# A linear/sliding-window attention stack with its backward pass: the dense backward stages rewritten with TensorE transposes, one fused first half and staggered tiles, weights loaded and transposed once

## The chip, the cores and the metric

The kernel runs on one core of one Trainium2 chip. The metric is device time in microseconds (us), as the median of the timed executions; less is better. A core has five engines that run their own instruction streams and wait for each other through semaphores: TensorE (PE, matmuls, with its weight loads shown apart as PEld), VectorE (DVE), ScalarE (ACT), GpSimd (POOL) and SyncE (SP). DMAs are started from the streams of SP, ACT and POOL and carried by 16 shared DMA engines; each stream works strictly in order, so a DMA or an instruction that waits holds up all that stands behind it on its engine. The row "PEclk" of the profile is the TensorE clock that was granted, as a share of full speed.

## The reference

A forward pass of four residual layers A, B, A, B over x of 2048 tokens by 640 features (32 heads of 20), and its gradients. Both kinds normalise, project to q, k, v, mix and project back; A and B have one set of weights each, used twice.

```
def _A_ref(x, wqkv, wo):                      # linear attention
    q, k, v = split_heads(x @ wqkv)
    phi = lambda t: jnp.where(t > 0, t + 1, jnp.exp(t)) + 1e-6
    pq, pk = phi(q), phi(k)
    kv = jnp.einsum("bhsd,bhse->bhde", pk, v)
    z = jnp.einsum("bhsd->bhd", pk)
    o = jnp.einsum("bhqd,bhde->bhqe", pq, kv) / (jnp.einsum("bhqd,bhd->bhq", pq, z)[..., None] + 1e-6)
    return merge_heads(o) @ wo
def _B_ref(x, wqkv, wo):                      # causal softmax attention, window of 256
    ...
x = A_x
x = x + _A_ref(_layernorm(x), A_wqkv, A_wo)
x = x + _B_ref(_layernorm(x), B_wqkv, B_wo)
x = x + _A_ref(_layernorm(x), A_wqkv, A_wo)
x = x + _B_ref(_layernorm(x), B_wqkv, B_wo)
outputs: x, d/dA_x, d/dA_wqkv, d/dA_wo, d/dB_wqkv, d/dB_wo for grad_out
```

## The kernel before, in words

Tokens are worked in 16 tiles of 128 rows (`TT`). All stages run one after the other on the core; the layers are numbered 0 (A), 1 (B), 2 (A), 3 (B). Within a stage the program is written tile by tile, and a scheduler that comes with the language lays each engine's instructions in an order of its own: it may move an instruction ahead of one that is written earlier if their data allow it.

1. Forward: `seg_first` does the first half of layer 0, then `seg_pair` twice does the rest of an A layer and the B layer behind it. Each `seg_pair` loads its weights anew (`load_w` for W and Wo of both kinds). `permute_w` writes a copy Wp of the B weights to DRAM at the very start.
2. `seg_do_first` (L645): for layer 3, dO = grad_out times the transposed Wo, scaled by row sums, and written to DRAM as rows (dO) and transposed (dOT). grad_out comes in transposed by DMA.
3. `seg_attention_bwd` (L666) of layer 3, then of layer 1: 128 units of 4 heads by 128 queries, each with two score products, exp, a mask on POOL, dS on DVE, half of the dS blocks transposed by TensorE and half by DMA, and three groups of products. In layer 1 the stage also carries the weight gradients of layers 3 and 2 (`wgrad`) as filler matmuls, `rate` of them at each of two places in a step; what is left over is drained after it. The results of a head group (16 tiles) are collected in one buffer `dqkv_o` and stored by one DMA; in layer 1 there is one such buffer, in layer 3 two.
4. The dense stages behind each attention. `seg_B_to_A` (L854): per tile, d(hn) = dqkv times the transposed Wqkv of B (`dh`, 30 matmuls of 320 columns), the backward of the normalisation, which updates the running gradient `car` in SBUF, then dO of the A layer below (`load_gT`, `A_do`, 10 matmuls), and every four tiles the products pq^T dN that sum into the gradient of the state (`band_products`, added up in SBUF by DVE). `seg_A_to_B` (L876): `close_A_bwd` masks that sum and transposes it, then per tile dq, dk, dv of the A layer (`A_dqkv`), `dh` with A's weights, and for layer 2 also dO of the B layer below (`B_do`). Every operand that a matmul needs transposed is transposed by DMA from the SP queue (`tr`): dqkv (15 blocks of 128 by 128), the gradient gT (5), dN (6), pk and v (5 each), the dO slab (8), and at the head of each stage the weights (75 blocks for Wqkv, 25 for Wo).
5. At the end the weight gradients of layers 1 and 0, added to those of 3 and 2.

The weights for step 4 are made by these lines, called in each dense stage:

```
elif name == "WT":
    t = pool.tile([P, self.QTT, D], BF, name=f"WT{kind}")
    self.tr(t, self.Wp if kind == 1 else self.Wqkv[kind])
```

## Time and profile before

| | |
|---|---|
| median of 3 executions | 2997.4 us (2982.85 to 3011.03) |
| the profiled execution, its own time | 2989.97 us |
| its span (first to last instruction) | 2988.3 us |
| mean granted TensorE clock | 0.794 |
| busy: PE, DVE, ACT, POOL | 2283.8, 1444.5, 1166.9, 765.0 us |
| DMA: packets, bytes | 1016354, 526.67 MB |

The stages in the profiled execution, by the first and last matmul of each: forward to 870 us, dO of layer 3 to 948 (its loads for the attention last to about 976), attention backward of layer 3 to 1353, its dense stages 1402 to 1804, attention backward of layer 1 from 1825 to 2390, left-over weight gradients to 2433, dense stages to 2768, last weight gradients from 2790 to the end. A window's line in the profile gives, after its length, the busy time of PE, PEld, DVE, ACT and POOL with the number of instructions, the granted clock, the mean busy share of the DMA engines (which may pass 1 where packets queue) and GB/s. In a line of waits stand the total, the number of times and the longest, in us.

### The profile page before, as it was taken

To read this page: it belongs to the slowest core of one execution; us is meant where nothing else is said; L and a number is where in the kernel's file an instruction comes from. 1 tells how busy PE (TensorE), PEld (TensorE's weight loads), DVE (VectorE), ACT (ScalarE), POOL (GpSimd) and SP (SyncE) were. 2 spreads that over 40 slices of the span, in tenths; PEclk is the share of its full clock that TensorE was granted. 3 is DMA by queue.
4 is the path that set the end of the run, shared out by engine and by line. 5 is a ranking of instruction groups with operands and counts; after the bars stand their busy time and mean duration, and the time that the engine had idled before them with its cause. 6 is when DMAs were issued, how large, how long until landed. Compare 5 with 4: busy or idle time off the path is not lost. (4 is left out here: it accounts for less than half of the span.)

```text
span 2988.3 us, 65913 instructions
## 1 busy us (share of the span) xinstructions
PE 2283.8 (76%) x26624; PEld 1393.9 (47%) x26624; DVE 1444.5 (48%) x3114; ACT 1166.9 (39%) x2161; POOL 765.0 (26%) x1282
## 2 busy tenths in 40 slices
PE   4689987499853899992746675996899868467689
PEld 3445654245431566662533342564566535244345
DVE  4455654344315666671754563554455427445212
ACT  3347765168740777770101112554555401011000
POOL 0124443146531333331221111222222212111000
PEclk9889997689956555555977785897899889678899
DMA  8698883799859777758978998678776598789776
GB/s 193 207 178 183 187 178 95 173 181 191 191 160 243 173 121 134 130 97 158 187 165 164 216 212 253 147 167 144 175 149 152 144 202 180 161 163 204 250 249 194
DMA packets 1016354, 526.67 MB, mean 176 GB/s; under 512 B 818928, under 2 KB 989936, under 8 KB 1014000
## 3 DMA queue, kind: packets, MB, share of 16 engines
q1 hardware_dynamic: 783984, 204.94, 42.6%
q10 hardware_dynamic: 221312, 280.80, 30.7%
q0 software_dynamic: 10752, 36.71, 5.2%
q8 instruction: 208, 3.41, 0.5%
q14 instruction: 98, 0.80, 0.1%
HBM read 187.40 MB, written 154.63 MB: 114 GB/s over the span
## 5 line engine op out<-in xcount | busy, mean ns | idle before, releaser
L746 DVE TENSOR_TENSOR ds<-sp,e 128x768 bf16<-128x768 f32 (+2 forms) x512 | 463.8, 906 | 418.1 <-PE sp L712 368.2
L726 ACT ACTIVATE e<-sp 128x768 bf16<-128x768 f32 (+2 forms) x512 | 394.7, 773 | 367.0 <-PE sp L712 258.8
L940 PE MATMUL wg<-wg_r,wg_l 128*128 128x320 bf16 (+1 forms) x2240 | 428.4, 336 | 98.5 <-DMA wg_r<-dqkv 32.6
L349 ACT ACTIVATE e<-s 128x768 bf16<-128x768 f32 (+2 forms) x512 | 372.7, 773 | 99.7 <-PE s L347 74.3
L577 PE MATMUL d<-WT,dqkvT 128*128 128x320 bf16 x1920 | 313.3, 328 | 126.6 <-DMA dqkvT<-dqkv_t 72.9
L730 POOL TENSOR_SCALAR_AFFINE_SELECT e<-e 128x512 bf16<-128x512 bf16 x256 | 162.6, 635 | 703.0 <-issue 538.9
L940 PEld LDWEIGHTS <-wg_l 128*128 128x128 bf16 x2240 | 213.7, 102 | 235.1 <-issue 91.3
L577 PEld LDWEIGHTS <-dqkvT 128*128 128x128 bf16 x1920 | 202.5, 107 | 225.3 <-DMA dqkvT<-dqkv_t 76.0
L352 POOL TENSOR_SCALAR_AFFINE_SELECT e<-e 128x512 bf16<-128x512 bf16 x256 | 162.9, 636 | 361.2 <-ACT e L349 357.6
L712 PE MATMUL sp<-KT,QT 32*128 32x384 bf16 (+2 forms) x1024 | 211.8, 411 | 47.1 <-DVE dO_t L533 15.3
L579 ACT ACTIVATE dh_junk<-d 128x320 bf16<-128x320 f32 x128 | 56.0, 437 | 476.9 <-PE d L577 471.8
L712 PE MATMUL sp<-VT,dOT 32*128 32x384 bf16 (+2 forms) x1024 | 212.2, 408 | 32.7 <-DMA dOT<-dOT 15.4
L522 PE MATMUL d<-WoT,gT 128*128 128x320 bf16 x640 | 121.8, 349 | 141.5 <-DMA gT<-car 109.2
L218 PE MATMUL d<-W,ln_hnT 128*128 128x320 bf16 x960 | 161.2, 323 | 56.6 <-DMA ln_hnT<-ln_hn 51.4
L203 PE MATMUL d<-Wo,oT 128*128 128x320 bf16 x640 | 129.8, 329 | 76.4 <-DMA Wo<-in_A_wo_dram 45.6
L306 PE MATMUL d<-W,ln_hnT 128*128 128x480 bf16 x640 | 178.8, 401 | 2.8 <-DVE o_t L293 2.7
L347 PE MATMUL s<-ring 32*128 32x128 bf16 x2880 | 158.0, 230 | 25.8 <-ACT e L349 25.0
L755 PE MATMUL tp<-ident,ds 128*128 128x128 bf16 x1440 | 168.5, 272 | 0.5
L581 DVE CUSTOM_DVE_ANT_0 dh_junk<-d,hn_ld 128x320 bf16<-128x320 f32 x128 | 62.3, 487 | 193.6 <-ACT dh_junk L579 193.4
L522 PEld LDWEIGHTS <-gT 128*128 128x128 bf16 x640 | 66.7, 110 | 189.6 <-DMA gT<-car 120.1
L767 PEld LDWEIGHTS <-ds 128*128 128x128 bf16 x2880 | 105.9, 101 | 100.5 <-issue 97.4
L355 POOL TENSOR_SCALAR_AFFINE_SELECT e<-e 128x512 bf16<-128x512 bf16 x224 | 144.9, 647 | 0.0
(123 smaller groups left out, 3424.5 us busy)
## 6 DMA issues: line engine op xcount, KB each, us to landing
qkvT<-ring ACTq DMA_DIRECT2D x32, 768.0 KB, 5.8
dqkv<-dqkv_o ACTq DMA_DIRECT2D x16, 960.0 KB, 6.1
dqkv<-dqkv_t ACTq DMA_DIRECT2D x32, 480.0 KB, 5.0
wg_r<-dqkv ACTq DMA_DIRECT2D x12, 1280.0 KB, 9.1
wg_r<-dqkv ACTq DMA_DIRECT2D x8, 1920.0 KB, 10.2
hn<-ln_hn ACTq DMA_DIRECT2D x64, 160.0 KB, 3.0
qk<-qk_flat ACTq DMA_DIRECT2D x64, 160.0 KB, 3.5
wg_l<-hn ACTq DMA_DIRECT2D x4, 2560.0 KB, 10.4
```

Source lines behind the costliest of these rows:

```text
L218: nc.tensor.matmul(ps, lhsT=hnT[:, k, :], rhs=W[:, k, ci * HD:(ci + 1) * HD], start=(k == 0), stop=(k == self.DT - 1))
L306: nc.tensor.matmul(ps, lhsT=hnT[:, k, :], rhs=W[:, k, ci * 480:(ci + 1) * 480], start=(k == 0), stop=(k == self.DT - 1))
L349: nc.scalar.activation(ev[:, 2 * half:2 * half + 2], ps[:, :, 0:nkt * P].rearrange("p h (i q) -> p h i q", q=P), ACT.Exp, scale=self.c_att)
L352: nc.gpsimd.affine_select(out=ev[:, :, nkt - 1, :], in_=ev[:, :, nkt - 1, :], compare_op=ALU.is_ge, fill=0.0, base=0, pattern=[[0, 4], [1, ...
L522: self.nc.tensor.matmul(ps, lhsT=gT[:, k, :], rhs=WoT[:, k, c * self.HD:(c + 1) * self.HD], start=(k == 0), stop=(k == self.DT - 1))
L577: nc.tensor.matmul(ps, lhsT=dT[:, k, :], rhs=WT[:, k, cs], start=(k == 0), stop=(k == self.QTT - 1))
L712: nc.tensor.matmul(ps[:, j, 0:nkt * P], lhsT=slabs[g][ta][r0:r0 + HP, b * P:(b + 1) * P], rhs=slabs[g][tb][r0:r0 + HP, k0 * P:(k0 + nkt) * P],
L726: nc.scalar.activation(ev[:, 2 * half:2 * half + 2], ps[:, :, 0:nkt * P].rearrange("p h (i k) -> p h i k", k=P), ACT.Exp, scale=c_att)
L730: nc.gpsimd.affine_select(out=ev[:, :, nkt - 1, :], in_=ev[:, :, nkt - 1, :], compare_op=ALU.is_ge, fill=0.0, base=0, pattern=[[0, 4], [-1 ...
L746: nc.vector.tensor_tensor(out=dv[:, hs], in0=ps[:, :, 0:nkt * P].rearrange("p h (i k) -> p h i k", k=P), in1=ev[:, hs], op=ALU.mult)
L755: nc.tensor.transpose(tp[:, i * P:(i + 1) * P], ds_of[u][:, (nb + i) * P:(nb + i + 1) * P], self.ident)
L940: nc.tensor.matmul(ps, lhsT=lhs[:, tt, rows], rhs=rhs[:, tt, 0:w], start=(tt == 0), stop=(tt == TT - 1))
```

## The change

- **Weights.** W and Wo of both kinds are loaded once, in `seg_first`, and kept for the forward pass. A new generator `flip_w` transposes the four weights once (10 DMA transposes of 15 blocks, 2 of 25) and writes them to DRAM (WT_d, WoT_d); the dense stages read them back with plain DMAs (`dense_weights`). `flip_w` is written as a side job of layer 3's attention; the weights' read follows it there, and in layer 1's attention it follows the filler.
- **Dense stages.** `seg_B_to_A` and `seg_A_to_B` become one function `seg_dense_bwd` with two loops. The gradient, dN, dq, dk/dv and the dO slab are transposed by TensorE against an identity matrix into PSUM (`flip`) and copied to SBUF, nearly all by ACT. Only dqkv of the B layer, pk and v are still transposed by DMA. dq of the A layer is made in the first loop, next to its dO, and the band sums stay in two PSUM banks over all 16 tiles. Each loop runs a plan of small steps at different tile offsets.
- **Work between engines.** The normalisation's backward (`ln_bwd`) reads PSUM once, by ACT (scaled, with the row sum), and goes on from SBUF; one addition and one multiplication of two tensors per tile go to POOL, which did none before; full-width operations (640) take the place of two halves (320).
- **Attention backward.** The factor c_att moves from the dO slab to the dS operation on DVE (tensor_tensor becomes scalar_tensor_tensor). `dqkv_o` becomes two half-size buffers, stored from the POOL queue. The filler rate in layer 1 goes from 5 to 6.

```
+    def flip_w(self, pool):
+        for kind, w in ((1, self.Wp), (0, self.Wqkv[0])):
+            t = pool.tile([P, self.QTT, D], BF, name="wt")
+            for k in range(DT):
+                self.tr(t[:, :, k * P:(k + 1) * P], w[k * P:(k + 1) * P, :])
+                yield
+            self.dma(self.WT_d[:, kind], t, self.nc.sync)
+            yield
...
+            self.tr(t[:, kind * DT:(kind + 1) * DT, :], self.Wo[kind])
...
+        self.dma(self.WoT_d, t[:, 0:2 * DT, :].rearrange("p (k d) f -> p k d f", k=2), self.nc.sync)
...
+    def flip(self, src, n, dst, pt, eng, first=0):
+        for i0 in range(0, n, 8):
+            k = min(8, n - i0)
+            tp = pt.tile([P, 1024], BF, name="t")
+            for i in range(k):
+                c = (first + i0 + i) * P
+                nc.tensor.transpose(tp[:, i * P:(i + 1) * P], src[:, c:c + P], self.ident)
+            v = tp[:, 0:k * P].rearrange("p (i q) -> p i q", q=P)
+            (eng[(i0 // 8) % len(eng)])(dst[:, i0:i0 + k, :], v)
...
         t = pw.tile([P, D], F32, name="do_o")
-        nc.vector.tensor_mul(t, dst, o)
+        nc.gpsimd.tensor_tensor(out=t, in0=dst, in1=o, op=ALU.mult)
...
+    def ln_bwd(self, l, tt, ps, hn, pw):
...
+        nc.scalar.activation(dhs.rearrange("p (c f) -> p c f", c=2), ps[:, :, 0:HD], ACT.Copy, scale=rs,
+                             accum_out=sm[:, 0:1])
...
+        nc.vector.tensor_tensor_reduce(out=junk, in0=dhs, in1=hn, scale=1.0, scalar=0.0,
+                                       op0=ALU.mult, op1=ALU.add, accum_out=sm[:, 1:2])
...
+        nc.gpsimd.tensor_tensor(out=u, in0=dhs, in1=g, op=ALU.add)
...
+        nc.vector.tensor_scalar_mul(ab, sm, -1.0 / D)
...
+        nc.scalar.activation(t2, hn, ACT.Identity, scale=ab[:, 1:2], bias=ab[:, 0:1])
+        nc.vector.tensor_add(g, u, t2)
...
-                nc.vector.tensor_tensor(out=dv[:, hs], in0=ps[:, :, 0:nkt * P].rearrange("p h (i k) -> p h i k", k=P),
-                                        in1=ev[:, hs], op=ALU.mult)
+                nc.vector.scalar_tensor_tensor(
+                    out=dv[:, hs], in0=ps[:, :, 0:nkt * P].rearrange("p h (i k) -> p h i k", k=P),
+                    scalar=c_att, in1=ev[:, hs], op0=ALU.mult, op1=ALU.mult)
...
-                if kt == TT - 1:
-                    self.dma(self.dqkv_d[l][:, :, g * 12 * DH:(g + 1) * 12 * DH], outs.pop(g))
+                if kt % OH == OH - 1:
+                    self.dma(self.dqkv_d[l][:, kt - OH + 1:kt + 1, g * 12 * DH:(g + 1) * 12 * DH], outs.pop(g),
+                             nc.gpsimd)
...
+    def dense_weights(self, l, pool):
+        w = [self.load_w(pool, 1, "WT"), self.load_w(pool, 0, "WoT"), pool.tile([P, 6, self.D], BF, name="mbdT")]
+        self.dma(w[2], self.sv[l - 1]["mbdT"])
+        return w
...
+                plan = ((fetch, 2), (dh0, 0), (flip_g, -1), (flip_dN, -2), (dh1, 0), (dO, -1), (dq_band, -2), (flip_dq, -3))
+                for s in range(-2, TT + 3):
+                    for f, d in plan:
+                        if 0 <= s + d < TT:
+                            f(s + d)
...
+                dmbd, dmbdT = self.close_A_bwd(bands, pb, pt)
...
+                tail = ((flip_g, -1), (dO, -1), (flip_dO, -2)) if a > 0 else ()
+                plan = ((fetch, 4), (fetch2, 2), (dh0, 0), *tail[:1], (flip_dkv, 1), (dh1, 0), *tail[1:2], (dkdv, 2),
+                        *tail[2:])
...
+                if l == 3:
+                    it = before(self.flip_w(self.pool(s3, "fwt", side="right")))
+                    self.seg_attention_bwd(l, None, 0, 3, side=it)
...
-                    self.seg_attention_bwd(l, it, 5, 2, 1)
-                    self.drain(it)
...
+                    it = before(both())
+                    self.seg_attention_bwd(l, it, 6, 2)
+                self.drain(it)
+                self.seg_dense_bwd(l, w)
```

In the plans, `fetch` starts a tile's loads and transposes, `dh0` and `dh1` are the two halves of `dh` (15 matmuls each), `dO` the 10 matmuls of dO with their DVE and POOL work, `dq_band` dq and the 10 band products, `dkdv` dk and dv, and the `flip` steps the TensorE transposes.

How the scheduler lays this, at two places. First the SP queue between the last forward tiles and the dO stage of layer 3; `oT<-o_b` is the last transposes of the forward pass, `gT` and `WoT` what the first matmul of the dO stage waits for. Before:

```order
L127 DMA_TRANSPOSE oT<-o_b 128x5x128 x4
L127 DMA_TRANSPOSE gT<-in_grad_out_dram 128x5x128 x2
L127 DMA_TRANSPOSE WoT_14160<-in_B_wo_dram 128x5x640
L127 DMA_TRANSPOSE gT<-in_grad_out_dram 128x5x128 x3
L127 DMA_TRANSPOSE dOT_ring_14158<-do_slab_14152 128x8x128
```

And now, where `wt` is the tile of `flip_w`:

```order
L129 DMA_TRANSPOSE wt<-Wp 128x15x128
L129 DMA_TRANSPOSE oT<-o_b 128x5x128
L129 DMA_TRANSPOSE wt<-Wp 128x15x128 x4
L129 DMA_TRANSPOSE WoT_14150<-in_B_wo_dram 128x5x640
L129 DMA_TRANSPOSE gT<-in_grad_out_dram 128x5x128
L123 DMA o_ld<-o_109 128x640
```

The first five transposes of `flip_w` stand ahead of WoT and gT. The other seven and the three stores of the transposed weights are spread over the same stage's gT transposes; behind the first dS transposition of the attention there is none.

Second, one tile on DVE in the first dense loop. Before (`dh` of one tile with `A_do` of the tile before it):

```order
L587 TENSOR_SCALAR dh_ab<-dh_ab,rs_97 128x2
L533 TENSOR_TENSOR dN<-d,rinv_100 128x320
L589 TENSOR_SCALAR dh_t_23602<-hn_ld,dh_ab 128x640
L537 TENSOR_TENSOR do_o<-dN,o_ld 128x640
L590 TENSOR_TENSOR car<-dh_t_23556,dh_t_23602 128x640
L539 TENSOR_REDUCE do_s<-do_o 128x32
L581 ISA dh_junk_23658,dh_sm<-d,hn_ld 128x320
```

And now, the whole step of a tile (`dh_s` is ACT's copy of the product, `dh_u` and `do_o` are made by POOL, `dh_t` by ACT):

```order
L595 ISA dh_junk,dh_sm<-dh_s,hn_ld 128x640
L595 ISA dh_sm 128x1
L558 TENSOR_TENSOR dN<-d,rinv_100 128x640
L600 TENSOR_SCALAR dh_ab<-dh_sm 128x2
L918 TENSOR_TENSOR dq_t<-d,dphi 128x640
L566 TENSOR_REDUCE do_s<-do_o 128x32
L603 TENSOR_TENSOR car<-dh_u,dh_t_23801 128x640
L894 CAST dN<-do_s 128x32
```

The reduction that waits for POOL's do_o now stands ahead of the addition into car, and the cast behind both.

413 lines of the change are left out of this document (224 added, 189 removed).

## The prediction

> **What bounds the kernel now.** I read the page first (PE busy 76% of the span, but its clock swings), then a table of the stages, then the waits inside the dense stages, then the timeline at their seams. The table: window, length, busy PE, PEld, DVE, ACT, POOL, granted clock, DMA share, GB/s.
>
> ```profile
> 870.00:948.00 78.00, 30.41 (x164) 16.99 (x166) 44.53 (x121) 0.00 (x0) 11.45 (x19) 0.74 0.93 232
> 948.00:1353.00 405.00, 370.39 (x6063) 236.49 (x6063) 258.79 (x329) 281.39 (x447) 147.03 (x240) 0.50 0.70 136
> 1353.00:1402.00 49.00, 0.52 (x9) 0.34 (x7) 0.00 (x0) 0.36 (x1) 5.51 (x11) 0.50 1.11 190
> 1402.00:1547.00 145.00, 106.20 (x801) 73.34 (x799) 102.60 (x260) 16.91 (x64) 28.59 (x57) 0.89 0.77 160
> 1547.00:1586.00 39.00, 7.60 (x46) 3.90 (x46) 5.96 (x16) 1.51 (x4) 6.97 (x13) 0.50 1.02 222
> 1586.00:1804.00 218.00, 152.40 (x948) 90.29 (x946) 126.46 (x362) 27.46 (x92) 28.22 (x52) 0.80 0.96 191
> 1825.00:2390.00 565.00, 494.21 (x7213) 305.16 (x7212) 273.58 (x349) 296.54 (x491) 147.17 (x241) 0.87 0.73 164
> 2390.00:2433.00 43.00, 21.10 (x118) 12.71 (x117) 1.48 (x3) 2.13 (x5) 5.31 (x10) 0.81 1.16 246
> 2433.00:2578.00 145.00, 108.81 (x800) 74.62 (x800) 101.86 (x260) 16.91 (x64) 26.52 (x54) 0.88 0.75 158
> 2578.00:2610.00 32.00, 7.77 (x44) 3.72 (x44) 5.85 (x15) 1.51 (x4) 5.32 (x10) 0.50 1.01 208
> 2610.00:2768.00 158.00, 114.31 (x788) 70.36 (x788) 79.45 (x231) 26.78 (x90) 23.96 (x38) 0.82 0.90 178
> ```
>
> The dense stages take 1353 to 1804 (451 us) and 2390 to 2768 (378 us). The seams (49, 39, 43 and 32 us) are nearly empty on every engine while the DMA engines are full. Inside, a tile takes 145/16 = 9.1, 218/16 = 13.6 and 158/16 = 9.9 us. What PE waits for there is transposed operands:
>
> ```profile
> PE d L577 <- DMA dqkvT<-dqkv: 48.5, 1, 48.5
> PE d L522 <- DMA gT<-car: 49.6, 12, 7.7
> PE d L577 <- DMA dqkvT<-dqkv_t: 25.1, 5, 9.1
> ```
>
> So the bound is the DMA transposition, in latency per tile and in weights per seam, and the change takes most of it away.
>
> **Forward.** The first output projection of each pair stands idle for a weight:
>
> ```profile
> 125.27 1.23 SPq L127 DMA_TRANSPOSE oT<-o_t  x1
> 142.62 2.83 PE L203 MATMUL d<-Wo,oT 128*128 128x320 bf16 x10 [23.47 <-DMA Wo<-in_A_wo_dram]
> 559.35 2.82 PE L203 MATMUL d<-Wo,oT 128*128 128x320 bf16 x10 [22.14 <-DMA Wo<-in_A_wo_dram]
> oT<-o_t SPq DMA_TRANSPOSE x32, 4.0
> ```
>
> With Wo there, what is late next is its other operand oT: issued at 125.3, 4.0 to landing, so 129.3 in place of 142.6, 13 us. The second wait is as long, so I take 13 again: **-26** (bounds -15, if the tiles behind it give half back, and -47, both waits whole). The earlier loads (4 MB more) stand behind x on the same queue at the start; I cost them at nothing, because the first matmul waits for W there too, and W now comes sooner.
>
> **dO of layer 3.** Written as a side job of the attention, `flip_w` is laid by the scheduler entirely in front of it: 5 transposes ahead of WoT and gT, 7 between the gT, three stores among them. 10 x 15 + 2 x 25 = 200 blocks; the price of one from
>
> ```profile
> 1541.46 16.74 SPq L127 DMA_TRANSPOSE WT<-in_A_wqkv_dram  x1
> q10 hardware_dynamic: 221312, 280.80, 30.7%
> ```
>
> 75 blocks in 16.74 us are 0.223 each: 45 us. The stores, twice 2.46 and once 1.64 MB, go at what the plain queue q10 shows: 280.8 MB in 30.7% of 2988 us are 306 GB/s: 21 us. Against these 66 us the stage has little room: its DMA share is 0.93, and 1.11 is the fullest that a seam shows, so 0.18 x 78 = 14 us. **+52**. Low: +22, if only half of the transposes' time lands on the path. High: +98, with 10 us of SP standing still behind each of two stores (the next `wt` reuses the tile) and the 3.3 MB of WT and WoT, 11 us, ahead of the attention's own rows on ACT's queue.
>
> **A step of the first dense loop.** Durations per instruction come from
>
> ```profile
> L579 ACT ACTIVATE dh_junk<-d 128x320 bf16<-128x320 f32 x128 | 56.0, 437 | 476.9 <-PE d L577 471.8
> L579 ACT ACTIVATION_READ_ACCUMULATOR dh_junk<-d 128x1 f32 x128 | 24.9, 194 | 0.0
> L761 ACT COPY dsT<-tp 128x768 bf16<-128x768 bf16 (+1 forms) x128 | 98.8, 772 | 31.4 <-PE tp L755 25.5 <-DMA po1w<-wg_o 0.9
> L590 DVE TENSOR_TENSOR car<-dh_t,dh_t 128x640 bf16<-128x640 f32 x64 | 52.2, 816 | 0.1
> L539 DVE TENSOR_REDUCE do_s<-do_o 128x32 f32<-128x640 f32 x64 | 52.0, 812 | 0.5
> L323 DVE COPY qk_flat<-qk_slab 128x640 bf16<-128x640 bf16 x64 | 25.8, 413 | 34.4 <-ACT qk_slab L316 34.0
> L598 DVE CAST dN<-do_s 128x32 bf16<-128x32 f32 x32 | 5.7, 177 | 0.3
> L730 POOL TENSOR_SCALAR_AFFINE_SELECT e<-e 128x512 bf16<-128x512 bf16 x256 | 162.6, 635 | 703.0 <-issue 538.9
> 1448.43 4.24 PE L577 MATMUL d<-WT,dqkvT 128*128 128x320 bf16 x30
> 1444.04 1.65 PE L577 MATMUL d<-WT,dqkvT 128*128 128x320 bf16 x11
> 1445.79 0.44 ACT L579 ACTIVATE dh_junk<-d 128x320 bf16<-128x320 f32 x1 [2.14 <-PE d L577]
> 1733.61 2.85 PE L522 MATMUL d<-WoT,gT 128*128 128x320 bf16 x10 [6.86 <-DMA gT<-car]
> 2380.51 0.51 PE L755 MATMUL tp<-ident,ds 128*128 128x128 bf16 x6
> 2747.03 0.30 PE L623 MATMUL d<-mbdT,dNT 32*128 32x320 bf16 x1
> 2749.25 4.24 PE L577 MATMUL d<-WT,dqkvT 128*128 128x320 bf16 x30
> ```
>
> PE's own work, at full clock: 40 matmuls of 320 columns at 4.24/30 = 0.141 are 5.65; 16 transposes at 0.51/8 = 0.06 (spacing, without the last one's tail) 1.0; dq 1.0 of the 2.2 us that dq, dk and dv take from 2747.03 to 2749.25; 10 band products 0.5, half of the 0.1 that those 22 matmuls average, as most have fewer columns: **8.1 us**.
>
> The step is not PE's, though. dN of tile t-1 must be transposed before `dh1` of the next tile, and DVE makes it behind work that needs `dh1` of this tile. The new wait is DVE's reduction for POOL's do_o; car and the cast are queued behind it, and PE's transposes of both, with `dh1` behind them, wait for these. The loop, from the end of one `dh1` to the end of the next: ACT's copy of 640 (between 437 for 320 and 772 for 768: 0.68) and its accumulator 0.19; DVE's product with hn 0.82; dN 0.82; POOL's do_o; the reduction 0.81; car 0.82; the cast 0.18; 11 transposes 0.65; 15 matmuls 2.12; eight changes of engine at 0.1 (PE's matmuls end at 1445.69, ACT begins at 1445.79). dq, the small ab and ACT's dh_t lie beside POOL's time. No row has a two-tensor operation on POOL. With one input, 635 ns for 512 make 0.79 for 640, and twice that is 1.6; below stands DVE's 0.82, above twice the 1.6, 3.2. I take 1.6, the row's price once per input: **9.5 us**. The page "GPSIMD Engine Reference" of the Trainium skill (section 3.1) gives 4497 ns for a two-tensor addition over 2048 on GpSimd against 2293 on VectorE; scaled to 640 that is an estimate of 1.4 us, by which the step would be 9.3. No run here shows it yet.
>
> **A step of the second loop.** For layer 2 the same chain with the slab's copy (0.41) in place of the cast and 15 transposes (0.9) in place of 11: 9.5 + 0.23 + 0.25 = **10.0**; PE's own 5.65 + 23 x 0.06 + 1.25 = 8.3. For layer 0 there is no dO and no such chain: PE's 30 x 0.141 + 10 x 0.06 + 1.25 = 6.1, plus a tenth for waits: **6.7**.
>
> **Seams.** The weights are in SBUF before the attention ends, so the first matmul waits for 15 blocks: 4.0 for the 5 of oT plus 10 x 0.22, about 7 us. Between the loops the last tile runs through its whole stagger: car (6.3 of the chain), its transposes and copy 1.0, dO 1.5, the dN chain 3.4, transposes, copy, dq and bands 2.6, five masked pieces with ACT copies of 0.77 about 5, dk, dv and their transposes 3.6, hops 1.6: 25 us.
>
> Layer 3's dense part: 7 + 16 x 9.5 + 25 + 16 x 10.0 + 9 for the last tile = 353, against 451: **-98**. Layer 1's: 7 + 152 + 25 + 107 + 3 = 294 against 378: **-84**.
>
> **Attention backward.** dS with its scalar costs the same by the two forms that the forward and dense stages have, and the stores of dqkv_o stop ACT:
>
> ```profile
> L229 DVE SCALAR_TENSOR_TENSOR pq_t<-d,phi_e 128x320 bf16<-128x320 f32 x64 | 30.7, 483 | 1.2
> L641 DVE TENSOR_TENSOR dqkv_t<-d,pk_l 128x320 bf16<-128x320 f32 x64 | 29.6, 481 | 21.4 <-PE d L634 21.4
> ACT dqkv_o L790 <- DMA dqkv<-dqkv_o: 31.3, 7, 7.3
> 2391.00:2427.00 36.00, 19.64 (x108) 11.98 (x108) 0.81 1.17 246
> ```
>
> Two half buffers give each store eight units of time, so that wait goes; PE, which runs on queued scores for part of it, gets perhaps two thirds back: **-20** (0 to -31). The left-over fillers, 108 recorded matmuls in the 36 us behind the stage, move into it at rate 6: 108 x 0.141 = 15, **+16** with their weights' first loads. The stores' issue moves to POOL, busy for 147 of 405 and 147 of 565 us there, so it hides beside the masks; without that cover 32 stores of a microsecond would be 32 us.
>
> Sum: -26 + 52 - 98 - 84 - 20 + 16 = -160. The profiled execution took 2990 (span 2988 and 2 around it): 2830. The median of the runs, 2997, lies 7 above it: 2837, rounded to **2840**.
>
> **Rivals.** *POOL slows the chain* (no change). do_o and dh_u run one after the other on POOL; at 3.2 us each do_o ends at 0.9 + 3.2 + 0.2 + 3.2 = 7.5 in place of 2.6 + 1.6 = 4.2, 3.3 us more in 48 steps, +158: 2998. For it: POOL had no such work, and each step has two DVE operations with two SBUF inputs beside it. Against: its one-input rows are steady. The page "GPSIMD Engine Reference" of the Trainium skill (section 1) lists the SBUF interfaces as shared with VectorE operations of two SBUF inputs, which would make this case likelier; no run here shows it. 0.09.
>
> *PE falls to half clock* (slower). Layer 3's attention runs at 0.50 with PE 91% busy, so being busy does not by itself keep the clock. Ten matmuls then took 2.85 (row of 1733.61) against 1.4 to 1.5 at full clock, 1.9 times: steps of 15.4, 15.8 and 11.6, PE-bound, +186 + 91 + 78 = 355 us: 3195. It decides from where some 45% of the dense time is cold. The Trainium skill, page "TensorE: Matmul & The Clock Gate", Part 4, says that transposes do not count as busy for the clock gate, and Part 1 that about 3.4 us of idling halves it; by that rule putting transposes on PE favours this rival. Against it here: the first loop before had 0.89 and 0.88 with PE idle for a quarter of the time, and in the new step PE rests about 1.5 us, plus 0.65 of transposes. 0.07.
>
> *The transposes of the weights flood the dO stage* by +98: 2886 or, with the attention's loads late as well, 2920. 0.13.
>
> *Everything overlaps better*: a step of 8.4, flips at their low bound: 2840 - 48 x 1.4 - 30 = 2743. 0.14.
>
> *The change doesn't do what it says*, for `flip_w`, is in the forecast already: moved beside the attention, it would be 2790.
>
> **Numbers.** The forecast has 0.54, 0.03 is left for mishaps of no name, on the slow side. About 1%, 30 us, can be told from no change. Faster: 0.54 + 0.13 + 0.14 and a little of the POOL case, 0.82; within 1%: 0.09; slower 0.09. The range leaves out the clock case and the ends: 2745 to 2970.
>
> **What would show it.** In the profile after: no PE wait for gT or dN from DMA; `t<-ident` transposes at about 0.06 spacing; a tile of the first loop every 9 to 10 us with PE waiting for DVE's car; POOL's TENSOR_TENSOR at 1.3 to 1.8 us; a clock above 0.85 in the loops; the seams at 5 to 10 and 20 to 30 us; the dO stage longer by some 50 us with `wt` on SP; Wo waits gone. POOL operations of 3 us, a clock near 0.5 in the loops, or a dO stage longer by 100 would make it wrong.

## The result, and the profile after

The changed kernel took a median of 2812.3 us (2805.3 to 2825.8) against 2995.4 for the kernel before beside it: a ratio of 0.939 (95% interval 0.933 to 0.945). The forecast was 2840 (2745 to 2970), with faster at 0.82. The profiled execution took 2815.3 us, its span is 2813.6, 174.7 less than before.

Stages are cut here by the first and last matmul of each, and the same cuts are used for every run below. "dO stage" is from the last output projection to the first product of layer 3's attention; a dense stage begins with the last product of the attention ahead of it.

| us | before | after | difference | predicted |
|---|---|---|---|---|
| forward | 870.0 | 848.3 | -22 | -26 |
| dO stage | 99 | 147 | +48 | +52 |
| attention, layer 3 | 384 | 385 | +1 | -20 and +16 in both attentions together |
| dense part of layer 3 | 451 | 353 | -98 | -98 |
| attention, layer 1 | 586 | 573 | -13 | (see layer 3's) |
| dense part of layer 1 | 378 | 284 | -94 | -84 |
| last weight gradients | 220 | 224 | +4 | 0 |

The table of windows of the kernel after (columns as before: window, length, busy PE, PEld, DVE, ACT, POOL, granted clock, DMA share, GB/s) has the dO stage, layer 3's attention, its first dense loop, the passage between the loops, its second loop, the filled part of layer 1's attention, and layer 1's two loops:

```profile
848.00:995.00 147.00, 43.73 (x186) 21.81 (x184) 43.69 (x85) 1.64 (x4) 26.69 (x21) 0.59 1.03 258
995.00:1379.80 384.80, 369.38 (x6042) 235.46 (x6041) 254.28 (x316) 278.77 (x443) 159.47 (x253) 0.50 0.69 135
...
1402.00:1540.00 138.00, 115.47 (x1047) 80.56 (x1047) 69.08 (x113) 53.30 (x84) 95.35 (x83) 0.97 0.55 149
1540.00:1568.60 28.60, 17.30 (x148) 12.47 (x146) 10.68 (x32) 11.03 (x15) 14.30 (x14) 0.67 0.56 179
1568.60:1732.50 163.90, 133.47 (x1197) 93.25 (x1195) 89.67 (x174) 76.99 (x109) 105.64 (x79) 0.98 0.59 160
...
1775.00:2306.00 531.00, 486.76 (x7289) 311.94 (x7286) 270.75 (x347) 292.02 (x488) 157.95 (x251) 0.92 0.78 169
...
2311.50:2470.40 158.90, 126.58 (x1107) 87.30 (x1107) 72.26 (x120) 55.06 (x88) 106.85 (x89) 0.96 0.60 156
2470.40:2496.00 25.60, 18.39 (x144) 12.35 (x145) 10.41 (x32) 10.99 (x15) 12.56 (x11) 0.65 0.49 99
2496.00:2589.60 93.60, 93.58 (x830) 66.49 (x827) 54.24 (x89) 51.21 (x75) 76.18 (x59) 0.99 0.67 174
```

In layer 3's dense part the first seam fell from 49 to 4 us, the first loop grew from 145 to 156 (it now also makes dq; the row of the table is its steady part, and its start, 1380 to 1402 us, ran at a clock of 0.73), the passage fell from 39 to 29, and the second loop from 218 to 164. The timeline of PE in the first loop shows the period, 9.46 us, by the transposes of car:

```profile
1515.24 0.45 PE L542 MATMUL t<-ident,car 128*128 128x128 bf16 x5 [1.54 <-DVE car L603]
...
1524.70 0.45 PE L542 MATMUL t<-ident,car 128*128 128x128 bf16 x5 [1.52 <-DVE car L603]
```

What makes the period is in the timelines of DVE and of POOL over the same step:

```profile
1519.08 0.82 DVE L595 CUSTOM_DVE_ANT_0 dh_junk<-dh_s,hn_ld 128x640 bf16<-128x640 f32 x1 [3.80 <-ACT dh_s L592]
...
1519.83 0.82 DVE L558 TENSOR_TENSOR dN<-d,rinv 128x640 bf16<-128x640 f32 x1
...
1522.67 0.82 DVE L566 TENSOR_REDUCE do_s<-do_o 128x32 f32<-128x640 f32 x1 [0.75 <-POOL do_o L564]
1523.40 1.24 DVE L603 TENSOR_TENSOR car<-dh_u,dh_t 128x640 bf16<-128x640 f32 x1
1524.56 0.17 DVE L894 CAST dN<-do_s 128x32 bf16<-128x32 f32 x1
```

```profile
1519.14 2.02 POOL L598 TENSOR_TENSOR dh_u<-dh_s,car 128x640 f32<-128x640 f32 x1 [2.35 <-ACT dh_s L592]
1521.11 0.17 POOL L893 MEMSET dN<- 128x96 bf16 x1
1521.24 1.39 POOL L564 TENSOR_TENSOR do_o<-dN,o_ld 128x640 f32<-128x640 bf16 x1
...
1523.25 2.34 POOL L916 TENSOR_SCALAR dphi<-pq_ld 128x640 bf16<-128x640 bf16 x1
```

dN ends at 1520.57 (where DVE's next operation begins), but do_o starts at 1521.24, when POOL is done with dh_u and a memset. And car takes 1.24 us, not 0.82, beside POOL's dphi.

The start and the forward (PE's timeline; the first row is the kernel before, the others after): the first matmul comes 8.9 us later. Where PE waited 23.5 and 22.1 us for Wo, it now waits 9.1 and 8.4, for oT.

```profile
35.37 2.05 PE L218 MATMUL d<-W,ln_hnT 128*128 128x320 bf16 x7 [35.37 <-DMA ln_hnT<-ln_hn]
```

```profile
44.25 2.05 PE L237 MATMUL d<-W,ln_hnT 128*128 128x320 bf16 x7 [44.25 <-DMA ln_hnT<-ln_hn]
136.26 2.85 PE L222 MATMUL d<-Wo,oT 128*128 128x320 bf16 x10 [9.05 <-DMA oT<-o_t]
537.44 2.85 PE L222 MATMUL d<-Wo,oT 128*128 128x320 bf16 x10 [8.43 <-DMA oT<-o_t]
```

ACT's queue at the start, before and after: in the kernel before, all eight reads of x stand ahead of everything, and the read of W follows at 24.35. In the kernel after, the read of W of A stands ahead of seven of the eight.

```profile
0.85 17.11 ACTq L121 DMA_DIRECT2D car<-in_A_x_dram  x8
```

```profile
1.33 0.48 ACTq L123 DMA_DIRECT2D W<-in_A_wqkv_dram  x1
1.84 27.98 ACTq L123 DMA_DIRECT2D car<-in_A_x_dram  x7
```

### The profile page after: what moved, and what is told of

It reads as the page before. It is cut to its first block, busy times and chain, and to the rows that moved or that the text cites. A ratio compares the mean times of both kernels' runs of the same rounds, so it can differ in the third digit from the quotient of the medians.

```text
span 2813.6 us, 67783 instructions
## 1 busy us (share of the span) xinstructions
PE 2282.4 (81%) x27724; PEld 1434.4 (51%) x27724; DVE 1324.4 (47%) x2474; ACT 1334.7 (47%) x2235; POOL 1102.8 (39%) x1410
## 5 line engine op out<-in xcount | busy, mean ns | idle before, releaser
L726 DVE SCALAR_TENSOR_TENSOR ds<-sp,e 128x768 bf16<-128x768 f32 (+2 forms) x512 | 464.2, 907 | 402.3 <-PE sp L692 317.0
L1047 PE MATMUL wg<-wg_r,wg_l 128*128 128x320 bf16 (+1 forms) x2240 | 408.5, 327 | 89.6 <-DMA wg_r<-dqkv 43.2
L325 PE MATMUL d<-W,ln_hnT 128*128 128x480 bf16 x640 | 170.5, 386 | 2.8 <-DVE o_t L312 2.7
L598 POOL TENSOR_TENSOR dh_u<-dh_s,car 128x640 f32<-128x640 f32 x64 | 118.4, 1851 | 121.4 <-ACT dh_s L592 121.1
L583 PE MATMUL d<-WT,dqkvT 128*128 128x320 bf16 x960 | 147.4, 308 | 17.8 <-DMA dqkvT<-dqkv 17.8
L237 PEld LDWEIGHTS <-ln_hnT 128*128 128x128 bf16 x960 | 93.3, 103 | 114.5 <-DMA ln_hnT<-ln_hn 63.3
L595 DVE CUSTOM_DVE_ANT_0 dh_junk<-dh_s,hn_ld 128x640 bf16<-128x640 f32 x64 | 61.2, 958 | 185.4 <-ACT dh_s L592 185.3
L366 PEld LDWEIGHTS <-ring 32*128 32x128 bf16 x2880 | 80.0, 96 | 122.8 <-issue 115.4
```

What stands on the lines that cost most here:

```text
L237: nc.tensor.matmul(ps, lhsT=hnT[:, k, :], rhs=W[:, k, ci * HD:(ci + 1) * HD], start=(k == 0), stop=(k == self.DT - 1))
L325: nc.tensor.matmul(ps, lhsT=hnT[:, k, :], rhs=W[:, k, ci * 480:(ci + 1) * 480], start=(k == 0), stop=(k == self.DT - 1))
L366: nc.tensor.matmul(ps[:, j, i * P:(i + 1) * P], lhsT=ring[r0:r0 + HP, G + g, kt * P:(kt + 1) * P], rhs=ring[r0:r0 + HP, g, qs], start=True ...
L583: self.nc.tensor.matmul(ps[:, c, 0:self.HD], lhsT=w, rhs=WT[:, k, c * self.HD:(c + 1) * self.HD], start=(k == 0), stop=(k == len(lhs) - 1))
L726: nc.vector.scalar_tensor_tensor(out=dv[:, hs], in0=ps[:, :, 0:nkt * P].rearrange("p h (i k) -> p h i k", k=P), scalar=c_att, in1=ev[:, hs ...
L1047: nc.tensor.matmul(ps, lhsT=lhs[:, tt, rows], rhs=rhs[:, tt, 0:w], start=(tt == 0), stop=(tt == TT - 1))
```

## The experiments

The table gives every run by the cuts above, with the ratio to runs of the kernel before made beside it (the kernels ran on several chips). "Steps" are times from car to car: the median in the first loop, and the mean of the 15 in layer 2's second loop, whose steps are uneven (10.1, 10.1, 9.0, 10.3 and again in the kernel after). The expectations quote the commonest step of that loop, 10.07. Layer 0's second loop has a median of 5.95 in all runs. Where nothing in them was changed, the forward varies by 844 to 856 us and layer 1's attention by 565 to 585, and with them the totals; the dense parts and the steps are the finer measure. Layer 1's attention goes with its granted clock: from its first score product to its last product it took 554 us at 0.910 (e2), 562 at 0.904 (after), 570 at 0.877 (e1) and 574 at 0.868 (e12).

| run | ratio (95%) | span | forward | dO stage | att. 3 | dense 3 | att. 1 | dense 1 | steps |
|---|---|---|---|---|---|---|---|---|---|
| after | 0.939 (0.933-0.945) | 2813.6 | 848 | 147 | 385 | 353 | 573 | 284 | 9.46, 9.57 |
| e1 dh_u on DVE | 0.928 (0.921-0.935) | 2796.8 | 844 | 150 | 384 | 343 | 581 | 270 | 8.90, 9.27 |
| e2 dphi on DVE | 0.925 (0.918-0.933) | 2780.9 | 844 | 147 | 385 | 343 | 565 | 273 | 9.05, 9.25 |
| e3 no flip_w | 0.923 (0.916-0.930) | 2779.8 | 849 | 108 | 384 | 355 | 574 | 286 | as after |
| e4 flip_w in attention | 0.926 (0.918-0.935) | 2774.3 | 845 | 107 | 400 | 353 | 568 | 279 | as after |
| e5 gT by DMA | 0.958 (0.953-0.962) | 2867.0 | 856 | 148 | 385 | 405 | 565 | 288 | 9.13, 11.98 |
| e6 weights at the seam | 0.934 (0.930-0.937) | 2803.1 | 847 | 117 | 383 | 364 | 580 | 293 | as after |
| e7 forward reloads | 0.953 (0.948-0.957) | 2859.3 | 947 | 100 | 383 | 355 | 570 | 280 | as after |
| e8 dqkv_o as before | 0.961 (0.957-0.965) | 2873.7 | 853 | 150 | 390 | 376 | 594 | 291 | as after |
| e9 later loads | 0.938 (0.934-0.943) | 2804.1 | 841 | 149 | 385 | 354 | 570 | 281 | as after |
| e10 e1 + e2 | 0.935 (0.930-0.939) | 2785.7 | 848 | 150 | 385 | 340 | 569 | 271 | 9.07, 9.04 |
| e11 e4 + e9 + e10 | 0.922 (0.919-0.926) | 2755.6 | 841 | 109 | 401 | 340 | 574 | 271 | 9.07, 9.02 |
| e12 later gT | 0.919 (0.915-0.923) | 2764.4 | 836 | 111 | 399 | 334 | 585 | 283 | 9.59, 7.91 |

### What POOL costs the step

**e1.**

```diff
-        nc.gpsimd.tensor_tensor(out=u, in0=dhs, in1=g, op=ALU.add)
+        nc.vector.tensor_tensor(out=u, in0=dhs, in1=g, op=ALU.add)
```

> The addition dh_u goes from POOL to DVE; nothing else. Theory, from the trace of the changed kernel: POOL is on the chain of the step, because dh_u (1.97 us) and a memset (0.13) stand ahead of do_o in its queue, so do_o starts 0.67 us after dN is there; with dh_u on DVE, where it fits between dq's product and the reduction, do_o starts when dN is there and a tile of the first loop falls from 9.46 to about 8.8 us, that of layer 2's second loop from 10.08 to about 9.4; 48 such steps: a span of 2813.6 - 31 = 2783. Rival, the chain as the prediction had it (DVE's product, then dN, then do_o, with dh_u beside it): the step stays at 9.5 or grows by up to 0.3 with DVE's load: 2813 to 2828.

The first loop's step fell to 8.90, as the theory had it: dh_u on POOL was on the chain. In layer 2's second loop the commonest step stayed at 10.04, but the mean fell from 9.57 to 9.27, half of what was expected. DVE's and POOL's timelines of e1 in the first loop show why the step fell no further than 8.90:

```profile
1478.89 1.52 DVE L603 TENSOR_TENSOR car<-dh_u,dh_t 128x640 bf16<-128x640 f32 x1
1480.33 0.81 DVE L566 TENSOR_REDUCE do_s<-do_o 128x32 f32<-128x640 f32 x1
```

```profile
1478.33 1.40 POOL L564 TENSOR_TENSOR do_o<-dN,o_ld 128x640 f32<-128x640 bf16 x1 [3.71 <-DVE dN L558]
```

With dh_u there early, the scheduler now lays car ahead of the reduction, where it runs beside do_o, and it takes 1.52 us.

**e2.**

```diff
-                    nc.gpsimd.tensor_scalar(out=f, in0=q, scalar1=-1e-6, scalar2=1.0, op0=ALU.add, op1=ALU.min)
+                    nc.vector.tensor_scalar(out=f, in0=q, scalar1=-1e-6, scalar2=1.0, op0=ALU.add, op1=ALU.min)
...
-                    nc.gpsimd.tensor_scalar(out=f, in0=pk.pop(t), scalar1=-1e-6, scalar2=1.0, op0=ALU.add, op1=ALU.min)
+                    nc.vector.tensor_scalar(out=f, in0=pk.pop(t), scalar1=-1e-6, scalar2=1.0, op0=ALU.add, op1=ALU.min)
```

> The two one-input operations dphi (clipping of pq and pk) go from POOL, where they take 2.34 us, to DVE. Theory: dphi is not waited for itself, but DVE's car in the first loop (1.23 us beside it against 0.82) and the copy into the dO slab in the second (0.73 against 0.41) are slowed by it; without it car is back at 0.82, the first loop's step falls by 0.4 (32 steps) and layer 2's second loop by 0.3 (16 steps): 2813.6 - 18 = 2796. Rival: car is slow for its own operands, the step stays at 9.46 and the span within 5 us of 2813.6. In either case DVE takes dphi in its idle 3.8 us of a step.

The first loop's step fell by 0.4 and the second's mean by 0.3, car is back at 0.82, and dphi takes 0.32 us on DVE. So POOL's dphi cost the step through DVE's operations beside it, although nothing waited for it. The two dense parts gave 20 us; the other 13 of the span lie in the forward and in layer 1's attention, which the edit doesn't touch and which vary by as much between runs.

**e10**, both together.

> dh_u and dphi both go from POOL to DVE (the first two runs together); POOL keeps do_o, a memset and the stores. Theory: the two gains have different places on the chain (the start of do_o; the length of car) and add: first loop 9.46 - 0.56 - 0.42 = 8.5, layer 2's second loop 10.07 - 0.8 = 9.3, since car there is no longer beside dphi either; 32 x 0.96 + 16 x 0.8 = 43: a span of 2770. Rival: the next bound is near (PE works 7.9 us of the 9.46, DVE has 1.5 us more to do), and the step stays at 8.9 and 9.6: 2790.

The rival's span was right, but not its reason for the first loop. There the step is 9.07, no better than with dphi alone: car again stands ahead of the reduction and beside do_o, at 1.51 us, and dphi between the reduction and the cast. What one edit frees there, the order gives back. In layer 2's second loop the commonest step is 9.62 as with dphi alone, yet the mean is 9.04 against 9.25, so that a little adds: the two dense parts take 611 us, against 613 in e1 and 616 in e2.

**e5.**

```diff
-                    self.flip(self.car[:, t, :], DT, gT[t], pt, [nc.scalar.copy])
+                    self.tr(gT[t], self.car[:, t, :])
```

> The gradient's transposition gT (5 blocks per tile, in both loops) goes back from TensorE and ACT to a DMA transpose on SP's queue; dN, dq, dk/dv and the dO slab stay on TensorE. Theory: car, gT, dO, dN, do_o, reduction, car of the next tile is a loop through all engines, so the 4 us of a DMA transpose stand in the step less the 2.8 us that PE works between car and dO, and less the 1.1 us that PE's transposes and ACT's copy take now: the first loop's step grows from 9.46 to 10.8 to 11.5, layer 2's second loop from 10.07 to 11.4 to 12; 48 steps of 1.3 to 2.0 make 62 to 96: a span of 2876 to 2910. Rival: PE's work between car and dO hides the DMA, and what the change won it won at the seams and by fewer operations: steps within 0.3 of now, 2813 to 2825.

In the second loop the theory held: the steps are very uneven (8 to 17 us), with a median of 11.6 and a mean of 12.0, and the loop grew by 36 us. In the first it failed: the median fell to 9.13, but some steps are 9.9 to 10.3, and from the third on they sum to 122.5 us against 123.0. So in the sum the DMA cost the steady first loop nothing and gave nothing. That the median fell because the transposes of car no longer stand on PE between car and dh1 is a guess. The loop's start made it 12 us longer: its second step took 27.8 us in place of 15.4, with PE waiting for the first gT. These two pieces make most of the 52 us by which layer 3's dense part grew. PE's waits in layer 3's two loops (total, times, longest):

```profile
PE d L550 <- DMA gT<-car: 82.1, 30, 20.9
```

The longest, 20.9, is the first tile's.

**e12**, on top of e9, e4 and e2:

```diff
-                plan = ((fetch, 2), (dh0, 0), (flip_g, -1), (flip_dN, -2), (dh1, 0), (dO, -1), (dq_band, -2), (flip_dq, -3))
+                plan = ((fetch, 2), (dh0, 0), (flip_dN, -2), (dh1, 0), (flip_g, -1), (dq_band, -2), (dO, -1), (flip_dq, -3))
...
-                plan = ((fetch, 4), (fetch2, 2), (dh0, 0), *tail[:1], (flip_dkv, 1), (dh1, 0), *tail[1:2], (dkdv, 2),
-                        *tail[2:])
+                plan = ((fetch, 4), (fetch2, 2), (dh0, 0), (flip_dkv, 1), (dh1, 0), *tail[:1], (dkdv, 2), *tail[1:])
```

> As the combined run (weights but W of A loaded later, flip_w in the attention, dphi on DVE), but dh_u stays on POOL, and in both loops' plans gT's transposes stand behind dh1 in place of ahead of it, with dq and the band products (first loop) or dk and dv (second) between them and dO. Theory, from the run with gT by DMA, where the first loop's step fell from 9.46 to 9.1: the 0.3 us of gT's transposes between car and dh1 lie on the loop car, dN's transposes, dh1, dh_s, car, and dO has time, since do_o waits for dh_u on POOL anyway: steps of 8.75 and 9.35 where dphi alone gave 9.05 and 9.65; 48 x 0.3 = 14 under the combined run: a span of 2741. Rival: dO, now behind dq, comes 1.5 us later, and dN, do_o and the reduction ahead of car with it: steps of 9.1 to 9.6 and a span of 2757 to 2780.

The first loop went the rival's way, with 9.59, and the span of 2764 lies in the rival's range. The second loop fell far below both: its commonest steps are 8.0 to 8.3 and its mean is 7.91, where dphi alone gave 9.25. What shortened it was not traced. DVE's and POOL's timelines of e12 in the first loop:

```profile
1441.83 2.01 DVE L606 TENSOR_TENSOR car<-dh_u,dh_t 128x640 bf16<-128x640 f32 x1
1443.77 0.81 DVE L569 TENSOR_REDUCE do_s<-do_o 128x32 f32<-128x640 f32 x1
```

```profile
1441.77 1.39 POOL L567 TENSOR_TENSOR do_o<-dN,o_ld 128x640 f32<-128x640 bf16 x1 [0.37 <-DVE dN L561]
```

car stands ahead of the reduction once more and now begins 0.06 us after do_o: 2.01 us. A plan with the new order in the second loop and the old one in the first was not run.

### The weights

**e3.**

```diff
-            self.dma(t, self.WT_d[:, kind])
+            self.dma(t.rearrange("p a f -> p (a f)"), (self.Wp if kind == 1 else self.Wqkv[kind]).rearrange("(p k) n -> p (k n)", p=P))
...
-                    it = before(self.flip_w(self.pool(s3, "fwt", side="right")))
+                    it = before(iter(()))
```

> The transposition of the weights (flip_w with its stores) is left out; the dense stages read the untransposed weights, as many bytes, so the gradients are not the reference's. Theory: the 200 blocks of transposes and 21 us of stores are the whole growth of the dO stage, from 99 us (last projection to first products of the attention) to 147; without them it is back at 99 to 110 (the weights' reads, 3.3 MB, still stand ahead of the attention's rows on ACT's queue): a span of 2765 to 2776. Rival: the stage is longer because of how the loads are ordered on the queues; then it stays above 130 us and the span above 2796.

The dO stage is 108 us, so flip_w's transposes and stores are 39 of its 48. Some 9.5 of the 39 lie at its end: in the kernel after, the first product comes 30.5 us after the last matmul of dO, in e3 21.0. ACT's queue in the kernel after shows what stands there:

```profile
966.67 0.33 ACTq L123 DMA_DIRECT2D WT<-WT_d  x1
981.82 0.54 ACTq L123 DMA_DIRECT2D dOT<-dOT_ring  x1
982.40 0.67 ACTq L123 DMA_DIRECT2D WoT<-WoT_d  x1
987.59 0.33 ACTq L123 DMA_DIRECT2D dOT<-dOT  x1
```

The store of the last dOT is not issued before 981.8, and the weights' reads stand on this queue ahead of the attention's own dOT. The other 9 us are there without flip_w. In e3 SP's transposition of Wo, which dO needs, waits 13.9 us (2.1 in the kernel before) until a store of output rows has landed, and this store was issued right behind the read of WT at 849 us. e7, below, which issues that read at 635, has a dO stage of 100. How much of the 9 is this wait in the kernel after, where flip_w's blocks hold SP at that time, can't be read from its trace.

**e4.**

```diff
+            self.att_pool = psl
...
-            t = pool.tile([P, self.QTT, D], BF, name="wt")
             for k in range(DT):
-                self.tr(t[:, :, k * P:(k + 1) * P], w[k * P:(k + 1) * P, :])
+                t = self.att_pool.tile([P, self.QTT, P], BF, name="dqkv_o")
+                self.tr(t, w[k * P:(k + 1) * P, :])
+                self.dma(self.WT_d[:, kind, :, k * P:(k + 1) * P], t, self.nc.sync)
                 yield
```

> flip_w takes its tiles (one block column at a time) from the rotating buffers of dqkv_o, so that its transposes cannot start before the attention of layer 3 has got that far and lie among its units. Theory: the DMA engines have room there (share 0.69 over 385 us) and PE sets the stage's pace at half clock, so the transposes cost nothing: dO stage about 100, attention 385 to 390, a span of 2765 to 2775. Rival: they hold up SP's queue, on which the attention's own dsT transposes stand behind them, and the attention grows by 20 to 45 us: 2785 to 2812.

In between: the dO stage fell by 40 and the span, 2774, is the theory's, but the attention grew by 15, to 400, and not by 0 to 5. The new wait is that for the attention's own transposes on SP's queue (PE's waits in the attention, e4, then the kernel after):

```profile
PE acc L751 <- DMA dsT<-ds: 14.7, 6, 3.7
```

```profile
PE acc L748 <- DMA dsT<-ds: 1.2, 2, 1.0
```

**e6.**

```diff
-            self.dma(t, self.WT_d[:, kind])
+            self.tr(t, self.Wp if kind == 1 else self.Wqkv[kind])
...
-            self.dma(t, self.WoT_d[:, kind])
+            self.tr(t, self.Wo[kind])
...
-                WTB, WoTA, mbdT = w
+                WTB, WoTA, mbdT = self.dense_weights(l, pb)
```

> flip_w is left out; the dense stages transpose their weights by DMA where they need them, behind the attention as the kernel before did, and everything else stays. Theory: the dO stage falls by 38 (as it did without flip_w), the seam behind layer 3's attention grows from 4 to about 49 and that behind layer 1's from 6 to 39 or more, and the second loop's 75 blocks hide beside the first loop: 2813.6 - 38 + 45 + 35 = 2855; the weights' part of the change is then worth some 40 us of its 177. Rival: the scheduler finds the transposes a place beside the attention, where the DMA engines have room: then the seams stay short and the span falls to 2775.

Both missed. The seams grew to 28 us only, by the wait

```profile
PE d L583 <- DMA WT<-Wp: 28.2, 1, 28.2
```

and half of that comes back: the first car follows the first product of the stage by 10 to 11 us in place of 19 to 22, and the dense parts are 11 and 9 longer. The dO stage is 30 shorter, but at 117 it is still 18 above the kernel before, with neither flip_w nor the reads of WT: six reads of rows now stand ahead on SP's queue, and the transposition of Wo holds it for 16.7 us, 9.0 in e3. In sum the span is 10 shorter than after, and the ratios overlap: transposing the weights once, where flip_w lies now, wins nothing over transposing them at each seam.

**e7.**

```diff
-            WA, WoA, WoB, WB = self.Wf
+            WB = self.load_w(pW, 1, "W")
+            WoA = self.load_w(pW, 0, "Wo")
+            WoB = self.load_w(pW, 1, "Wo")
             last = l + 2 > 3
+            WA = None if last else self.load_w(pW, 0, "W")
...
```

> The forward pass loads its weights anew in each part, as the kernel before did, and keeps none; the rest of the change stays. Theory: the first matmul comes at 35 us in place of 44 (the kept weights' 4 MB stand ahead of Ln on ACT's queue), the two waits for Wo come back with about 30, so that the forward ends 22 later, at 870; but the kept weights' SBUF is free then, flip_w moves ahead into the forward, where the DMA engines have room (0.76), and the dO stage falls from 147 to 100-108: 2813.6 + 22 - 40 = 2796. Rival: the flips cost in the forward what they cost in the dO stage, and the span is 2830 to 2840; or the Wo waits are not what the kept weights win, and the forward ends where it does now or earlier.

The rival's direction was right, but the span of 2859 is above its 2840 too. The first matmul is back at 36 us and the dO stage at 100, but the forward ends at 947, 77 later than in the kernel before, which loads its weights the same way. What is new in it is flip_w with its stores and, behind it, the read of WT: the kept weights' SBUF is free, and the scheduler lays them there (waits of PE, 0 to 950; two stretches of SP's timeline and one of ACT's):

```profile
PE d L222 <- DMA oT<-o_t: 83.9, 9, 32.4
...
PE d L222 <- DMA Wo<-in_A_wo_dram: 51.2, 2, 27.8
```

```profile
547.52 20.39 SPq L129 DMA_TRANSPOSE wt<-Wp  x4
...
637.20 37.63 SPq L129 DMA_TRANSPOSE ring<-v_slab  x1
```

```profile
635.25 0.33 ACTq L123 DMA_DIRECT2D WT<-WT_d  x1
```

SP stands for 20 us on four weight transposes and later for 38 on one of the forward's own, and the oT behind them on that queue come late: PE waits 84 us for oT, 27 in the kernel before. The 38 us fall together with the read of WT, which is issued at 635.25 and lands 42 us later (9 to 10 us in other runs), while the DMA engines move 85 GB/s at a busy share of 1.25 (637 to 675 us). So about half of the 77 falls together with that read and is not the transposes' alone, and no run has this forward without flip_w. The waits for Wo, 51 us here, 46 in the kernel before and none after, confirm what the kept weights win.

**e9.**

```diff
-            self.Wf = (W, self.load_w(pf, 0, "Wo"), self.load_w(pf, 1, "Wo"), self.load_w(pf, 1, "W"))
...
             for tt in range(self.TT):
+                if tt == 6:
+                    self.Wf = (W, self.load_w(pf, 0, "Wo"), self.load_w(pf, 1, "Wo"), self.load_w(pf, 1, "W"))
```

> Wo of both kinds and W of B are loaded behind the sixth tile's normalisation instead of at the very start; they are still loaded once. Theory: the 4 MB cost the start 8 to 9 us, because ACT's first Ln stands behind their issues and the issues wait for queue slots (first matmul at 44 us, 35 before the change); without them the first matmul comes at 35 to 37 and the forward ends 8 earlier, at 840: a span of 2806. Rival: the first matmul waits for W and x, whose bytes are the same, or a later wait takes the gain back: forward end at 846 to 850, 2813.

The first matmul comes at 39.8, not 36: W of A still stands ahead of x, and e7, which has it behind x, starts at 35.9. The forward ends at 841, near the 840 that were expected, but only 4.4 us of this lie at the start; what gave the rest was not traced, and 841 is 3 us below the shortest forward of the runs that leave it alone. In the total this is too small to tell (0.938).

### The results of a head group

**e8.**

```diff
-                if kt % OH == 0:
-                    outs[g] = psl.tile([P, OH, 12 * DH], BF, name="dqkv_o")
+                if kt == 0:
+                    outs[g] = psl.tile([P, TT, 12 * DH], BF, name="dqkv_o", bufs=1 if fill else 2)
...
-                if kt % OH == OH - 1:
+                if kt == TT - 1:
```

> The results of a head group are collected and stored as the kernel before did (one buffer of 16 tiles in layer 1, two in layer 3, one DMA on ACT's queue); the rest of the change stays. Theory: layer 1's attention, 573 us from the last dense matmul to its last product, waits again for the store (31 us in the kernel before, two thirds of them on the path): 587 to 594; layer 3's attention stays at 385, since PE at half clock sets its pace: a span of 2827 to 2835. Rival: PE has queued work for the time of that wait, and the double buffer won nothing: both attentions as now within 8 us, 2806 to 2822.

Layer 1's attention is 594, as the theory had it, and layer 3's 390, 5 more. The clock has a part in the 594: at like clocks (e8 at 0.875, e1 at 0.877) the stretch from first score product to last product is 583 against 570, so that about 13 of the 21 us are the buffers'. ACT waits 18.6 us there for the store, none in the kernel after. The larger part of the loss lies elsewhere: the seams are 20 us in place of 4 and 6, because the first dqkvT must wait for the store of a whole group (PE, 1385 to 1420 us):

```profile
PE d L583 <- DMA dqkvT<-dqkv: 20.2, 1, 20.2
```

Layer 3's dense part is 23 longer, layer 1's 8. In all the old buffers take back 60 of the 175 us that the change won. The edit also moves the stores from POOL's queue back to ACT's, and no run tells the two apart.

### All that won, together

**e11.** 

> The three together: weights but W of A loaded behind the sixth tile, flip_w in the attention of layer 3, dh_u and dphi on DVE. Theory: each stands in another stage, so the gains add: 8 + 39 + 43 = 90: a span of 2724, some 9% under the kernel before. Rival: they share ACT's and SP's queues at the seams and half of one is lost: 2740 to 2750.

Some two thirds of the sum came: 58 us of the 90 by the span, which at 2756 is just above the rival's range. The dO stage (109), the forward (841) and the dense parts (340 and 271) each keep what they won alone. What the sum had wrong is that the attention pays 15 for flip_w, and that e10's gain is not the 43 that the sum took but 26 in the dense parts. The median is 2761.3 us (2757.3 to 2776.9), the ratio 0.922; e12 has 2762.2 and 0.919 (0.915 to 0.923). Both beat the kernel before by 8%, and by their ratios the changed kernel by about 2%.

## Why the prediction was right, point by point

**The time, 2840 measured 2812.** Of the 28 us, 15 are in the sum (mainly layer 0's second loop and layer 1's attention); 13 come from the step from the profiled execution to the median, which was put 7 above it and lay 3 below, and from rounding.

**Forward, -26 measured -22.** The two waits shortened by 14.4 and 13.7 us, where the sum had 13 each. "Costed at nothing", because the loads stand behind x and the first matmul waits for W, was the step that failed: the first matmul comes 8.9 us later. It waits for ln_hnT, and ACT's first Ln, which that needs, comes at 31.55 us in place of 24.77, behind the issues of these loads. About half of the delay goes with the three weights that are loaded early, by e9 (39.8 in place of 44.25); the other half goes with W of A, which now stands ahead of x, by e9 and e7 (39.8 against 35.9). Some 2.5 us of the gain were not traced; runs that leave the forward alone differ by more.

**dO of layer 3, +52 measured +48.** The sum came near, its parts less so, which is partly luck. flip_w is 39 by e3, where the sum had 45 + 21 - 14 = 52; 9 more are there without flip_w, which the prediction had only in its upper bound, at 11. By the prediction's own cut, which ends at the first score product, the stage grew by 39 (78 to 117), and the attention of layer 3 by 9.

**A step of the first loop, 9.5 measured 9.46; of layer 2's second, 10.0 measured 10.07 for the commonest and 9.57 in the mean.** The numbers came near, the chain was partly wrong, and that its errors cancelled is luck. That PE's transposes wait for car, and car for POOL's do_o and the reduction, holds. But the part from ACT to do_o goes over POOL's dh_u and memset (2.1 us), not over DVE's product and dN (1.6); e1, which takes dh_u off POOL, has 0.56 us less in the step, net of the new order. car took 1.16 to its successor where 0.82 stood, and e2 gives that back. Against these stood do_o, 1.39 where 1.6 was taken, and smaller things. The POOL rival was thus at work in small: POOL's queue, not do_o's price, and 0.6 us of dh_u's, which takes 1.4 where it began first and 2.0 beside DVE's dh_junk. For do_o an estimate of 1.4 had been worked out from the page "GPSIMD Engine Reference" of the Trainium skill (section 3.1); the trace agrees, 1.39 and 1.42.

**Layer 0's second loop, 6.7 measured 5.95.** The mis-sized term: the loop was put at 110 us and took 93.6. That is 16 too many, against which the first loop ahead of it took 159 where 152 stood; so layer 1's dense part came out 10 under the sum. PE's own 6.1 was right and the tenth for waits too much; PE is busy for 93.58 of 93.60 us.

**Seams and passages, 7, 25 and 9 measured 4 to 6, 26 to 29 and 5.** Right in sum. That layer 3's dense part came out at 353 as forecast is partly luck: the seam took 3 less, the first loop 4 more (its second step is 15.4), the passage 4 more and the second loop 5 less. The price of 7 moreover rested on something that the sum booked under the attention: without the half buffers of dqkv_o the seam is 20 (e8).

**Attention, -20 and +16 measured +1 and -13.** In layer 3 the half buffers gave at most the 5 us of e8; PE ran there at 0.50 of its clock and was busy for 96% of the time. In layer 1 they gave about 13 by e8 at a like clock. Of the stage's -13, 10 lie between the last dense matmul and the first score product (21 us before, 11 after), and the rest is no larger than what the clock changes between runs; so what the fillers cost or gave, where +16 stood for them, is not shown. dS cost the same in both forms, 907 ns against 906 in the kernel before:

```profile
L726 DVE SCALAR_TENSOR_TENSOR ds<-sp,e 128x768 bf16<-128x768 f32 (+2 forms) x512 | 464.2, 907 | 402.3 <-PE sp L692 317.0
```

**The rivals.** Half clock: the loops ran at 0.96 to 0.99, and only the start of a loop and the passages at 0.65 to 0.73, so it was wrong. The rule of the Trainium skill, page "TensorE: Matmul & The Clock Gate", Part 4, that transposes do not count as busy in the same way, did no harm here: the longest waits for car in the steady loop are 1.5 us, with many matmuls between; the runs don't test the rule itself. The flood of the dO stage: half of its 98. Better overlap: not by itself, but e12's second loop, with a mean of 7.91, shows that its step of 8.4 was within reach there; in the first loop no run came below 8.90. Two prices in the rivals are slightly off by the prediction's own steps: half clock makes 189 + 93 + 78 = 360 where 355 stands, and better overlap 61 for the 48 steps where 48 x 1.4 = 67 stands; and the seam's 4.0 + 2.2 is 6.2 where about 7 stands. None of them changes an outcome.

**What the prediction did not ask** is which part of the change wins. Most is in the dense loops and in the short stores. The single transposition of the weights, which gave two terms of the sum, shows no gain in the place where the scheduler put it (e6).

## What to carry to other kernels

A DMA queue that works in order is a resource of its own: the same transposes of the weights went with 77 us in the forward, 39 in the dO stage and 15 in the attention, by what stood behind them on that queue. (The load of the DMA engines differed too, and in the forward the read of WT had a large part, so the three numbers are not the price of the queue alone.) When work goes to another engine, follow its queue and its neighbours too: the addition that "lay beside" the chain delayed the one on it, and an operation that nobody waited for slowed two that were waited for. And when a step is cut, read the new order before adding gains up: in e1, e10 and e12 the scheduler moved car beside do_o.
